# Unit 10's state sums and scores in block 3's third visit, and two visits in block 4

## The chip, the core and the metric

The kernel runs on one core of one Trainium2 chip. The core has five engines with a queue each: TensorE (PE in the profile), VectorE (DVE), ScalarE (ACT), GpSimd (POOL) and SyncE (SP), which here issues almost all DMAs. The metric is the device time of one execution in microseconds (us). Before the change its median over three runs is 198.28 us (198.15 to 198.75).

## The reference

Two stages follow each other. The first is a recurrent attention with decay (4 batches, 8 heads, 768 steps, heads of 64), the second a two-layer network with a PReLU (3072 tokens, width 512, inner width 2048):

```python
for t in range(S):
    state = gamma[None, :, None, None] * state + np.einsum('bhd,bhe->bhde', k[:, :, t], v[:, :, t])
    y[:, :, t] = scale * np.einsum('bhd,bhde->bhe', q[:, :, t], state)
...
x = np.ascontiguousarray(attn_out.transpose(0, 2, 1, 3)).reshape(B * S, H * D)
...
h = x @ w_in
g = np.maximum(h, 0.0) + alpha * np.minimum(h, 0.0)
return (g @ w_out).astype(np.float32)
```

## The kernel before

The tokens are cut into 12 units of 256 (three to a batch), and two units make a block of 512 tokens, so blocks 0 to 5. The attention of a unit is done in chunked form: products of k and v give the sums that move the state on (state sums), products of k and q give the scores within a chunk, which are masked, and then both are applied (`halves_out`) to give the unit's output y, which ScalarE copies from PSUM into `xT`, the input of the network.

Everything is ordered by hand: each engine runs its queue in the order in which the code emits it. For block n, the first layer is a generator `ffn1(n)` of 16 turns. A turn is four matmuls (128x512) into one PSUM bank, a ReLU on ScalarE into `hm` (three buffers) and a `scalar_tensor_tensor` on VectorE into `gt`. Turns alternate between the lower and the upper half of the inner width: turn 14 makes `gt[7]`, turn 15 `gt[15]`. After turn 7 and after turn 15, VectorE makes sums of `gt` (`g_sums`), two instructions each time, for a second layer that needs seven products instead of eight (`ffn2_seven`, a generator of 7 x 16 matmuls of 128x256; the products are called ox and oy after their banks). `tick(gen, m)` emits the next m matmuls of a generator with what belongs to them.

The loop over n (line 1188 on) runs the first layer of block n with the preparation of the next block's units u0 = 2(n+1) and u1 = u0 + 1 beside it, and then the second layer of block n with the attention of these two units in between. The preparation of a unit is, on GpSimd, two rescales (k and q, from float32 to float16 with the decay, `rescale`) and a cast of v (`cast_v`); on SyncE's queue a transposing DMA (`turn_dma`), the next loads (`load`, four DMAs each for k and v, one for q) and two small DMAs that move half of q (`move_q`). The first rescale is made to wait (`behind`) for the last sum of `gt` of the block before (`gate`).

From unit 6 on (`MID`), the attention goes to TensorE in three visits, small matmuls of 64x64 tiles between the large ones:

1. after 16 matmuls of the second layer: the state sums of both units (`halves_mm`) and the scores of u0 (`half_mm`);
2. after 40 more: the output of u0 (`halves_out`) and the scores of u1;
3. after 24 more: the output of u1. Then `begin(n + 1)` emits the first four matmuls of the next block's first layer; in its first turn `ffn1` takes the two units one at a time, so that these four need only u0's output. The 32 matmuls that remain of the second layer follow.

Between the visits VectorE and GpSimd carry the state on (`middle`, `behind_middle`), VectorE masks the scores (`half_masks`), and GpSimd and ScalarE copy the states to where the matmuls read them (`middle_copy`, `state_copy`; part 0 is GpSimd's, part 1 ScalarE's). Block 2 has units 6 and 7, block 3 units 8 and 9, block 4 units 10 and 11. Block 5 has no units beside it and a first layer of its own (`ffn1_mixed`).

In the trace, L632 are the first layer's matmuls, L857 the second layer's, L284 the state sums, L345 the scores, L384 and L398 the outputs; L648 and L650 are a turn's ReLU and PReLU, L613 the sums of `gt`; L185, L201 and L205 are rescale, cast and transpose; L159 and L165 the loads, L220 `move_q`; L301, L312, L313 the state, L356 the masks; L329, L333, L450, L452 the copies; L881 an addition at the end of a product.

Of the kernel before, what the change touches and what calls it, by code (L numbers as in the profile page):

```python
# [22 lines left out]
def kernel(  # L23
# [22 lines left out]

    SPLIT = 4
    MID = 6
    U = 256
    UPB = S // U  # L50
    NU = B * UPB
# [130 lines left out]
    def rescale(eng, u, t, h0, h1):  # L182
        kdq = unit(u)[0]
        at = OQ if t else (O2 if u >= SPLIT else 0)
        return eng.tensor_tensor(  # L185
            out=kdq[:, t, :, h0:h1, :].rearrange("p r h d -> p h r d"),
            in0=staged[u]["kq"[t]][:, h0:h1, :].rearrange("p h (r d) -> p h r d", r=2),
            in1=tab[:, at + 2 * h0 : at + 2 * h1]
            .rearrange("p (h r) -> p h r", r=2)
            .unsqueeze(3)  # L190
            .to_broadcast([128, h1 - h0, 2, D]),
            op=MULT,
        )
# [419 lines left out]
        last_g.append(nc.vector.tensor_tensor(out=o, in0=a, in1=b, op=op))  # L613
        return last_g[-1]

    def ffn1(n, banks, apart=0):


        turns = [(f, 2, ul, ul + 1) for ul in range(2) for f in range(0, apart, 2)]
        rest = range(apart, NFT)  # L620
        if apart == 0:
            rest = [f + x for f in range(HF) for x in (0, HF)]
        turns += [(f, 1, 0, 2) for f in rest]
        gt = None
        for i, (f0, nf, lo, hi) in enumerate(turns):
            hps = ps(banks[i % len(banks)], "hps").rearrange("p (f t) -> p f t", f=nf)
            parts = [(f, lo, hi) for f in range(nf)]
            if n > 1 and i == 0:
                parts = [(0, 0, 1), (0, 1, 2)]
            for f, ul, uh in parts:  # L630
                for hp in range(4):
                    nc.tensor.matmul(  # L632
                        out=hps[:, f, U * (ul - lo) : U * (uh - lo)].rearrange(
                            "p (u t) -> p u t", t=U
                        ),
                        lhsT=w_in_all[:, hp, 128 * (f0 + f) : 128 * (f0 + f) + 128],
                        rhs=xT[n][:, ul:uh, hp, :],
                        start=(hp == 0),
                        stop=(hp == 3),
                    )  # L640
# [7 lines left out]
            nc.scalar.activation(out=hm, in_=hps, func=RELU, bias=0.0, scale=-1.0)  # L648
            for f in range(nf):
                nc.vector.scalar_tensor_tensor(  # L650
                    out=gt[:, f0 + f, U * lo : U * hi],
                    in0=hm[:, f, :],
                    scalar=oma_sb[:, f0 + f : f0 + f + 1],
                    in1=hps[:, f, :],
                    op0=MULT,
                    op1=ADD,
                )
# [520 lines left out]
    BANKS5 = (7, 4, 7, 3, 6, 0, 4, 7)  # L1178

    def begin(n):  # L1180
        if n + 1 < NBLK:
            gen = ffn1(n, (6, 2, 3, 1, 0, 7, 5, 4, 6, 1, 0, 4, 5, 7, 6, 1))
        else:
            gen = ffn1_mixed(n, PLAN5, BANKS5)
        tick(gen, 4)
        return gen

    for n in range(1, NBLK):
        more = n + 1 < NBLK
        u0 = 2 * (n + 1)  # L1190
        if n > 1:
            gen = begun
            if more:
                for u in (u0, u0 + 1):
                    i = rescale(G, u, 0, 0, 8)
                    if u == u0:
                        behind(i, gate)
                    rescale(G, u, 1, 0, 8)
                    turn_dma(u)
                    cast_v(G, u)  # L1200
                    if u > u0:
                        load(u + 1, "qv")
                    else:
                        load(u + 2, "k")
                    move_q(u)
                    tick(gen, 8)
            tick(gen)
            if not more:
                for i in (2, 4):
                    for lo in (0, 4):  # L1210
                        g_sums(n, i, lo, lo + 4)
                g_sums(n, 0, 0, HF)
                g_sums(n, 3, 0, HF)
        gen = ffn2_seven(n, 0, 1) if more else ffn2_seven(n, 0, 1, (2, 3, (4, 6)))
        if more and u0 >= MID:
            u1 = u0 + 1
            tick(gen, 16)
            halves_mm(u0, (2, 3))
            halves_mm(u1, (6, 7))
            half_mm(u0, (4, 5))  # L1220
            m00 = middle(u0, 0)
            s00 = behind_middle(m00)
            half_masks(u0, 0)
            state_copy(s00, part=0)
            m01 = middle(u0, 1)
            s01 = behind_middle(m01)
            state_copy(s01, part=0)
            tick(gen, 8)
            middle_copy(m00, 1)
            state_copy(s00, part=1)  # L1230
            middle_copy(m01, 1)
            tick(gen, 9)
            half_masks(u0, 1)
            m10 = middle(u1, 0)
            s10 = behind_middle(m10)
            state_copy(s10, part=0)
            load(u0 + 3)
            g_sums(n, 2, 0, HF)
            tick(gen, 15)
            state_copy(s01, part=1)  # L1240
            middle_copy(m10, 1)
            tick(gen, 8)
            halves_out(u0, (2, 3))
            half_mm(u1, (4, 5))
            half_masks(u1, 0)
            state_copy(s10, part=1)
            m11 = middle(u1, 1)
            middle_copy(m11, 1)
            half_masks(u1, 1)
            s11 = behind_middle(m11)  # L1250
            state_copy(s11, part=0)
            gate = g_sums(n, 3, 0, HF)
            tick(gen, 24)
            halves_out(u1, (4, 5), evict=False)
            begun = begin(n + 1)
            take_y(u1, (0, 1))
            state_copy(s11, part=1)
            if n == NBLK - 2:
                in_sums(6, 0, V)
                in_sums(6, 1, V)  # L1260
                x_sums(n + 1, V)
                in_sums(4, 0, V)
                in_sums(4, 1, V)
        elif more:
            tick(gen, 16)
            sum_mm(u0, (2, 3))
            sum_mm(u0 + 1, (2, 3), half=1)
            score_mm(u0, 0, (4, 5))
            score_mm(u0, 1, (6, 7))
# [24 lines left out]
            state_copy(s11, part=1)  # L1294
            masks(u0 + 1, 0)
            masks(u0 + 1, 1)
            gate = g_sums(n, 3, 0, HF)
            tick(gen, 24)
            out_mm(u0 + 1, (4, 5), evict=False)
            begun = begin(n + 1)  # L1300
            take_y(u0 + 1, (0, 1))
        tick(gen)
        if n == NBLK - 2:
            in_sums(6, 2, V)
            in_sums(6, 3, V)
            in_sums(4, 2, V)
            in_sums(4, 3, V)
# [30 lines left out]
```

## Time and profile before

| | before |
|---|---|
| median of 3 runs (lowest to highest) | 198.28 us (198.15 to 198.75) |
| the profiled execution: its time | 198.86 us |
| its span, first to last instruction | 196.9 us |
| busy: TensorE, VectorE, ScalarE, GpSimd | 189.3, 156.3, 115.4, 106.1 us |
| granted TensorE clock, mean | 0.997 |
| block 3: first layer of the block / second layer with visits | 111.09 to 124.48 / 124.48 to 139.98 us |
| block 4: the same | 139.98 to 153.37 / 153.37 to 168.84 us |

The page gives busy times and shares for the whole span; the chain of waits follows the work that ended last back from its last instruction, and shows block after block when TensorE was at which line; a timeline lists the instructions of one engine in order, neighbours of one kind merged ("x8"), with the engine's idle time before them and what ended it. In rows of the timeline the first number is the start within the span, the second the duration, both in us; TensorE's starts there are about 0.17 us ahead of those of the chain, which counts from the end of the matmul before.

### The profile page before, as it was taken

Reading aid. Unit: us, or ns where it says so; the run is one execution under the profiler, and the core shown is the slowest. Engines: PE = TensorE matmul, PEld = TensorE weight load, DVE = VectorE, ACT = ScalarE, POOL = GpSimd, SP = SyncE. Lnnn points to the kernel's source line nnn. Section 1 sums busy time; section 2 is a strip of 40 time slices with the busy share of each in tenths; the row PEclk is TensorE's granted clock in tenths of the full one; section 3 lists DMA queues with packets and bytes.
Section 4 is the critical chain, followed back from the end, with each engine's and each line's share of the span. In section 5 each row is a group of like instructions: output and inputs, shape, how many; then the busy total and the mean of one; then the engine's idle time right before and its main releaser. Section 6 shows DMA issues by size and latency. Waiting matters only on the chain.

```text
span 196.9 us, 6085 instructions
## 1 busy us (share of the span) xinstructions
PE 189.3 (96%) x2529; PEld 128.8 (65%) x2529; DVE 156.3 (79%) x259; ACT 115.4 (59%) x199; POOL 106.1 (54%) x113
## 2 busy tenths in 40 slices
PE   6688999999999999999999999999999999999993
PEld 2356645568467688744688744788644788865882
DVE  7698987517698998289988389977489996999983
ACT  4458665349187668467467476467466486678110
POOL 3176897499549544970077980076970180039300
PEclk9999999999999999999999999999999999999998
DMA  5999999998879989898988899929865010400014
GB/s 156 313 317 380 374 381 377 293 180 136 211 192 200 286 197 265 213 311 175 213 203 209 256 201 191 222 65 225 256 122 126 17 57 3 160 3 0 0 65 152
DMA packets 90026, 37.92 MB, mean 193 GB/s; under 512 B 57984, under 2 KB 87696, under 8 KB 90000
## 3 DMA queue, kind: packets, MB, share of 16 engines
q1 hardware_dynamic: 88768, 36.45, 69.2%
q0 software_dynamic: 1056, 1.05, 3.6%
q8 instruction: 20, 0.33, 0.6%
q10 hardware_dynamic: 176, 0.04, 0.1%
q14 instruction: 6, 0.05, 0.1%
HBM read 27.31 MB, written 6.29 MB: 171 GB/s over the span
## 4 chain that ended last, share of the span: by engine, by line
PE 90%; SPq 4%; DMA 3%; DVE 0%; issue 0%; POOL 0%; DVEq 0%
PE hps L632 36%; PE ox L857 16%; PE oy L857 12%; PE ops L809 7%; SPq L165 4%; PE hps L719 4%; PE sp L761 3%; DMA vs<-in_v_dram 3%; PE y L533 1%; PE y L384 1%; PE trb L230 1%; PE st L284 1%; PE sca L466 1%; PE ov L857 1%; PE ow L857 1%; PE oz L857 1%
## 5 line engine op out<-in xcount | busy, mean ns | idle before, releaser
L632 PE MATMUL hps<-xT,win 128*128 128x512 f16 (+1 forms) x396 | 71.5, 338 | 0.3 <-DVE ss L423 0.3
L650 DVE SCALAR_TENSOR_TENSOR gt<-hm,oma,hps 128x512 f16<-128x512 f32 (+1 forms) x96 | 59.4, 656 | 12.1 <-issue 4.3
L648 ACT ACTIVATE hm<-hps 128x512 f32<-128x512 f32 x80 | 47.6, 597 | 24.6 <-PE hps L632 22.5
L632 PEld LDWEIGHTS <-win 128*128 128x128 f16 x396 | 38.1, 98 | 31.0 <-POOL win L978 0.4
L857 PEld LDWEIGHTS <-gs 128*128 128x128 f16 x320 | 31.0, 98 | 3.7
L857 PEld LDWEIGHTS <-gt 128*128 128x128 f16 x240 | 22.9, 98 | 4.0
L333 POOL CAST tg<-tm 64x256 f16<-64x256 f32 x12 | 4.8, 396 | 34.3 <-DVE tm L301 22.3
L185 POOL TENSOR_TENSOR kdq<-qs,tab 128x1024 f16<-128x1024 f32 (+1 forms) x12 | 20.2, 1686 | 3.0 <-DVE wsum L572 2.3
L185 POOL TENSOR_TENSOR kdq<-ks,tab 128x1024 f16<-128x1024 f32 (+1 forms) x12 | 20.2, 1686 | 2.6 <-PE y L515 2.6
L857 PE MATMUL ox<-wout,gt 128*128 128x256 f16 x144 | 17.3, 273 | 0.0
L857 PE MATMUL oy<-wsum,gs 128*128 128x256 f16 x144 | 17.2, 273 | 0.0
L556 ACT ACTIVATE xT<-y 128x512 f16<-128x512 f32 x22 | 14.9, 744 | 3.1 <-PE y L533 2.0
L201 POOL CAST vx<-vs 128x1024 f16<-128x1024 f32 (+1 forms) x13 | 12.6, 970 | 6.7 <-DMA vs<-in_v_dram 6.7
L809 PE MATMUL ops<-wout,gt 128*128 128x512 f16 x64 | 15.3, 380 | 0.0
L613 DVE TENSOR_TENSOR gs<-gt 128x1024 f16<-128x1024 f16 (+1 forms) x14 | 13.0, 934 | 0.2
L877 ACT ACTIVATE cu<-oy 128x512 f32<-128x512 f32 x10 | 6.0, 597 | 10.6 <-PE oy L857 10.1
L236 ACT ACTIVATE kq<-trb 128x1024 f16<-128x1024 f16 x8 | 8.2, 1023 | 6.3 <-PE trb L230 6.3
L313 POOL TENSOR_TENSOR tf<-ss,tab 128x256 f32<-128x256 f32 x10 | 10.3, 1028 | 2.5 <-DVE ss L312 1.3
L881 DVE TENSOR_TENSOR os<-ox,cu 128x512 f32<-128x512 f32 x5 | 3.4, 687 | 10.1 <-PE ox L857 10.1
L670 POOL TENSOR_SCALAR hn<-qc,oma 128x256 f32<-128x256 f32 x4 | 4.5, 1138 | 12.4 <-DVE qc L785 12.3
L809 PEld LDWEIGHTS <-gt 128*128 128x128 f16 x64 | 5.8, 98 | 6.0
L424 POOL TENSOR_TENSOR tf<-ss,tab 128x256 f32<-128x256 f32 x6 | 5.9, 980 | 7.1 <-DVE ss L423 7.1
(119 smaller groups left out, 293.1 us busy)
## 6 DMA issues: line engine op xcount, KB each, us to landing
qs<-in_q_dram SPq DMA_DIRECT2D x9, 512.0 KB, 5.4
ks<-in_k_dram SPq DMA_DIRECT2D x32, 128.0 KB, 3.5
vs<-in_v_dram SPq DMA_DIRECT2D x32, 128.0 KB, 4.6
early<-in_moe_w_in_dram SPq DMA_DIRECT2D x7, 512.0 KB, 7.5
out_dram<-os SPq DMA_DIRECT2D x9, 256.0 KB, 2.5
early<-in_moe_w_out_dram SPq DMA_DIRECT2D x4, 512.0 KB, 7.0
out_dram<-ot SPq DMA_DIRECT2D x4, 512.0 KB, 3.8
ks<-in_k_dram SPq DMA_DIRECT2D x6, 256.0 KB, 6.1
```

What stands on the lines that cost most here:

```text
L165: nc.sync.dma_start(out=t[nm[0]][:, h, :], in_=src[b, h, U * c : U * c + U, :].rearrange("h (p r) d -> p h (r d)", r=2),)
L185: return eng.tensor_tensor(out=kdq[:, t, :, h0:h1, :].rearrange("p r h d -> p h r d"), in0=staged[u]["kq"[t]][:, h0:h1, :].rearrange("p h ...
L201: eng.tensor_copy(out=o, in_=i)
L236: nc.scalar.activation(out=kq.rearrange("p (x a) i -> p x a i", x=4)[:, :, 2 * hh : 2 * hh + 2, :], in_=trb.rearrange("p (x a i) -> p x a ...
L313: nc.gpsimd.tensor_tensor(out=t, in0=ss, in1=dec, op=MULT)
L556: nc.scalar.activation(out=o, in_=i, func=COPY, bias=0.0, scale=1.0,)
L613: last_g.append(nc.vector.tensor_tensor(out=o, in0=a, in1=b, op=op))
L632: nc.tensor.matmul(out=hps[:, f, U * (ul - lo) : U * (uh - lo)].rearrange("p (u t) -> p u t", t=U), lhsT=w_in_all[:, hp, 128 * (f0 + f) : ...
L648: nc.scalar.activation(out=hm, in_=hps, func=RELU, bias=0.0, scale=-1.0)
L650: nc.vector.scalar_tensor_tensor(out=gt[:, f0 + f, U * lo : U * hi], in0=hm[:, f, :], scalar=oma_sb[:, f0 + f : f0 + f + 1], in1=hps[:, f, :],
L809: nc.tensor.matmul(out=opss[tq], lhsT=gt[:, ft, 128 * tq : 128 * tq + 128], rhs=w_out_all[:, ft, :], start=(ft == 0), stop=(ft == NFT - 1),)
L857: nc.tensor.matmul(out=o[1][m], lhsT=lhs(f, m), rhs=rhs(f), start=(first and f == 0 and (m == 0 or o[0] is None)), stop=(f == HF - 1), ski ...
```

## The change

Units in `AHEAD` (only unit 10) are prepared one block earlier. In block 2, `load(10, "kq")` follows unit 9's loads. Beside block 3's first layer GpSimd rescales and casts units 8, 9 and 10 (`prepare`), with unit 10's v loaded there. In block 3's third visit, unit 10's scores come ahead of unit 9's output and its state sums behind, and the state work and masks of unit 10 (`first_half`) follow on the other engines; block 4's first layer is not begun there, and its first turn is not split. Block 4 prepares unit 11 alone and has two visits: the output of unit 10 with unit 11's state sums and scores after 16 matmuls of the second layer, and the output of unit 11 after 64 more. Blocks 1, 2 and 5 keep their order but for the loads. The visits as they were are now the function `visits`, left out here.

```diff
+    AHEAD = (10,)
...
-    def ffn1(n, banks, apart=0):
+    def ffn1(n, banks, apart=0, early=False):
...
-            if n > 1 and i == 0:
+            if early and i == 0:
                 parts = [(0, 0, 1), (0, 1, 2)]
...
     def begin(n):
+        if 2 * n + 2 in AHEAD:
+            return ffn1(n, (4, 5, 6, 1, 0, 2, 3, 7, 6, 1, 0, 4, 5, 7, 6, 1))
         if n + 1 < NBLK:
-            gen = ffn1(n, (6, 2, 3, 1, 0, 7, 5, 4, 6, 1, 0, 4, 5, 7, 6, 1))
+            gen = ffn1(n, (6, 2, 3, 1, 0, 7, 5, 4, 6, 1, 0, 4, 5, 7, 6, 1), early=True)
...
+    def prepare(u0, gate):
+        def scaled(u, gate=None):
+            i = rescale(G, u, 0, 0, 8)
+            if gate is not None:
+                behind(i, gate)
+            rescale(G, u, 1, 0, 8)
+            turn_dma(u)
+
+        far, u1 = u0 + 2, u0 + 1
+        if u0 in AHEAD:
+            scaled(u1, gate)
+            cast_v(G, u1)
+            move_q(u1)
+            yield
+            return
+        scaled(u0, gate)
+        cast_v(G, u0)
+        load(far, "v" if far in AHEAD else "k")
+        move_q(u0)
+        yield
+        scaled(u1)
+        cast_v(G, u1)
+        if far in AHEAD:
+            yield
+            scaled(far)
+            cast_v(G, far)
+        else:
+            load(far, "qv")
+        move_q(u1)
+        yield
+
+    def vnext(u0):
+        if u0 + 2 in AHEAD:
+            move_q(u0 + 2)
+        load(u0 + 3)
+        if u0 + 4 in AHEAD:
+            load(u0 + 4, "kq")
...
+    def first_half(u):
+        m0 = middle(u, 0)
+        s0 = behind_middle(m0)
+        half_masks(u, 0)
+        state_copy(s0, part=0)
+        m1 = middle(u, 1)
+        s1 = behind_middle(m1)
+        half_masks(u, 1)
+        state_copy(s1, part=0)
+        return m0, s0, m1, s1
...
+                for _ in prepare(u0, gate):
                     tick(gen, 8)
+                    state_copy(begun_state.pop() if begun_state else None, part=1)
...
+            if u0 in AHEAD:
+                halves_out(u0, (2, 3))
+                halves_mm(u1, (4, 5))
+                half_mm(u1, (6, 7))
+                m10, s10, m11, s11 = first_half(u1)
+                tick(gen, 17)
+                vnext(u0)
+                middle_copy(m10, 1)
+                state_copy(s10, part=1)
+                middle_copy(m11, 1)
+                g_sums(n, 2, 0, HF)
+                tick(gen, 15)
+                state_copy(s11, part=1)
+                s11 = None
+                gate = g_sums(n, 3, 0, HF)
+                tick(gen, 32)
+            else:
+                s11 = visits(n, gen, u0)
+                gate = g_sums(n, 3, 0, HF)
+                tick(gen, 24)
+            ahead = u0 + 2 in AHEAD
+            if ahead:
+                half_mm(u0 + 2, (6, 7))
+            halves_out(u1, (4, 5), evict=ahead)
+            if ahead:
+                halves_mm(u0 + 2, (2, 3))
+                state_copy(s11, part=1)
+                m00, s00, m01, s01 = first_half(u0 + 2)
+                begun = begin(n + 1)
+                tick(gen)
+                middle_copy(m00, 1)
+                state_copy(s00, part=1)
+                middle_copy(m01, 1)
+                begun_state.append(s01)
+            else:
+                begun = begin(n + 1)
+                take_y(u1, (0, 1))
+                state_copy(s11, part=1)
```

More of the change, by code (lines that the diff above doesn't have):

```diff
@@ L1186, in begin, with visits @@
         return gen
+    def prepare(u0, gate):
[33 more added lines that the diff above has]
+            load(u0 + 4, "kq")
+    begun_state = []
+    def first_half(u):
[8 more added lines that the diff above has]
+        return m0, s0, m1, s1
+    def visits(n, gen, u0):
+        u1 = u0 + 1
+        halves_mm(u0, (2, 3))
+        halves_mm(u1, (6, 7))
+        half_mm(u0, (4, 5))
+        m00 = middle(u0, 0)
+        s00 = behind_middle(m00)
+        half_masks(u0, 0)
+        state_copy(s00, part=0)
+        m01 = middle(u0, 1)
+        s01 = behind_middle(m01)
+        state_copy(s01, part=0)
+        tick(gen, 8)
+        middle_copy(m00, 1)
+        state_copy(s00, part=1)
+        middle_copy(m01, 1)
+        tick(gen, 9)
+        half_masks(u0, 1)
+        m10 = middle(u1, 0)
+        s10 = behind_middle(m10)
+        state_copy(s10, part=0)
+        vnext(u0)
+        g_sums(n, 2, 0, HF)
+        tick(gen, 15)
+        state_copy(s01, part=1)
+        middle_copy(m10, 1)
+        tick(gen, 8)
+        halves_out(u0, (2, 3))
+        half_mm(u1, (4, 5))
+        half_masks(u1, 0)
+        state_copy(s10, part=1)
+        m11 = middle(u1, 1)
+        middle_copy(m11, 1)
+        half_masks(u1, 1)
+        s11 = behind_middle(m11)
+        state_copy(s11, part=0)
+        return s11
     for n in range(1, NBLK):
@@ L1217 @@
             tick(gen, 16)
[L1218 to L1247, printed above, removed]
```

32 lines of the change are left out of this document (10 added, 22 removed).

## The prediction

> **What bounds the kernel now.** I read the page's busy shares first, then the chain that ended last, then the timelines of VectorE, GpSimd and the DMA queue around block 3.
>
> ```profile
> span 196.9 us, 6085 instructions
> PE 189.3 (96%) x2529; PEld 128.8 (65%) x2529; DVE 156.3 (79%) x259; ACT 115.4 (59%) x199; POOL 106.1 (54%) x113
> ks<-in_k_dram SPq DMA_DIRECT2D x32, 128.0 KB, 3.5
> vs<-in_v_dram SPq DMA_DIRECT2D x32, 128.0 KB, 4.6
> ```
>
> TensorE is busy 96% of the span, and the chain of waits runs through it almost without a break from block 1 on. So the change can win only what it takes off TensorE's own sequence, and loses whatever makes TensorE wait. Rows of the chain in blocks 3 and 4 (start, duration, what):
>
> ```profile
> 111.09 13.39 PE hps L632 x64
> 124.48 1.78 PE ox L857 x16
> ...
> 127.16 1.85 PE ox L857 x16
> 129.02 1.75 PE oy L857 x16
> ...
> 135.32 0.27 PE y L384 x17
> ...
> 135.94 0.54 PE hps L632 x4
> ...
> 155.15 0.56 PE st L284 x49
> ...
> 156.02 1.85 PE ox L857 x16
> ...
> 160.49 0.38 PE y L384 x32
> ...
> 161.43 0.98 PE ox L857 x8
> ...
> 164.15 0.39 PE y L384 x32
> ...
> 164.80 0.54 PE sp L761 x4
> ```
>
> These show the three attention visits of block 4, cut into the products of the second layer: they last from 155.15 to 156.02, 160.49 to 161.43 and 164.15 to 164.80. The group of large matmuls behind each visit is about 0.10 longer than the same group elsewhere (1.85 against 1.75 for 16; 0.98 for eight, where half of 1.75 is 0.87).
>
> The second thing to see is how closely the first product of a block follows VectorE. VectorE's timeline at the end of block 3's first layer, one instruction of it by itself, and TensorE's timeline just behind:
>
> ```profile
> 119.02 0.69 DVE L613 TENSOR_TENSOR gs<-gt 128x1024 f16<-128x1024 f16 x1
> 119.75 0.69 DVE L613 TENSOR_TENSOR gs<-gs,gt 128x1024 f16<-128x1024 f16 x1
> 120.36 5.54 DVE L650 SCALAR_TENSOR_TENSOR gt<-hm,oma,hps 128x512 f16<-128x512 f32 x8
> ```
>
> ```profile
> 124.31 0.74 DVE L650 SCALAR_TENSOR_TENSOR gt<-hm,oma,hps 128x512 f16<-128x512 f32 x1
> ```
>
> ```profile
> 125.10 0.39 PE L857 MATMUL ox<-wout,gt 128*128 128x256 f16 x2
> ```
>
> Turns 8 to 15 of the PReLU follow the two sums of `gt` (the two `g_sums` after turn 7) back to back, 0.66 apart from 120.36. Turn 14 writes `gt[7]` and ends at 124.31 + 0.74 = 125.05. The eighth matmul of the first product takes `gt[7]` as weights and starts at 125.10. It already waits: the group takes 1.78 where its like take 1.75. So there is no slack; whatever delays VectorE between 119.0 and 125.0 is time lost on TensorE, one to one.
>
> **The change, part by part.** *One visit fewer.* From the code, block 4's visits hold 32 + 24 + 32 = 88, 64 + 32 = 96 and 64 small matmuls, in 0.87, 0.94 and 0.65. Slope (0.94 - 0.65) / 32 = 0.009 each, and 0.65 - 64 x 0.009 = 0.07 fixed. With the 0.10 that the next group loses, a visit costs 0.17 besides its matmuls. Unit 10's 64 matmuls (state sums and scores) move unchanged: block 3's third visit (0.62, from 135.32 to 135.94) grows by 0.58, and block 4 gets visits of 120 and 64. Gain: 0.17.
>
> *No early start of block 4's first layer.* The first turn is no longer split in eight matmuls of 256 columns, but four of 512: the same columns, so nothing. What it covered was unit 9's eviction, on ScalarE in block 3 before:
>
> ```profile
> 136.14 1.34 ACT L556 ACTIVATE xT<-y 128x512 f16<-128x512 f32 x2 [0.19 <-PE y L398]
> ```
>
> The 32 matmuls of the second layer that remain behind the visit (2 x 1.75 = 3.5) cover these 1.34; without them TensorE would wait about that long.
>
> *VectorE and ScalarE, moved.*
>
> ```profile
> L301 DVE TENSOR_TENSOR tm<-tf,st 128x256 f32<-128x256 f32 x10 | 4.2, 417 | 1.0 <-POOL tf L313 1.0
> L356 DVE TENSOR_TENSOR m<-sca,mi 128x512 f16<-128x512 f32 x6 | 4.1, 688 | 1.1 <-PE scb L345 1.1
> ```
>
> ```profile
> 140.02 0.69 DVE L881 TENSOR_TENSOR os<-ox,cu 128x512 f32<-128x512 f32 x1 [3.34 <-PE ox L857]
> ```
>
> Unit 10's two middles and two sums (0.42 each) and two masks (0.69) are 3.1 on VectorE, in the hole of 3.34 in which it waited for the last product of block 3. ScalarE's extra copies lie there too. Without that hole the first turns of block 4 would come up to 3 late, and TensorE would wait for banks. I take nothing.
>
> *The DMA queue.* k and q of unit 10 go out behind unit 9's loads in block 2.
>
> ```profile
> 101.92 2.70 SPq L159 DMA_DIRECT2D ks<-in_k_dram  x4
> 104.66 0.62 SPq L165 DMA_DIRECT2D qs<-in_q_dram  x1
> 105.33 4.03 SPq L159 DMA_DIRECT2D vs<-in_v_dram  x4
> ```
>
> ```profile
> DMA to landing us min/median/max: 4.8/5.4/6.7
> ```
>
> The last row is for all loads of q. Unit 10's four k loads are issued from 109.4, 0.67 each, q at 112.1; block 2's two stores and unit 8's transpose stand 3.3 later in the queue. With 3.5 to land (page) k is there at about 115.6, q between 116.9 and 118.8. Unit 8's transpose, issued near 113.6 instead of 112.3, is needed by TensorE near 126.8. `move_q(9)` moves behind unit 10's transpose, which waits for GpSimd until about 121.5; it is needed at 135.3. v of unit 10 takes the place that k had. In block 3 `move_q(10)`, two issues of about 0.65, pushes unit 11's loads back 1.3; GpSimd takes them up only from about 140.5. All hidden.
>
> *GpSimd.* This is the step that costs. Before, its timeline is:
>
> ```profile
> 107.83 1.90 POOL L185 TENSOR_TENSOR kdq<-ks,tab 128x1024 f16<-128x1024 f32 x1
> ...
> 116.24 1.03 POOL L201 CAST vx<-vs 128x1024 f16<-128x1024 f32 x1
> 127.74 0.39 POOL L333 CAST tg<-tm 64x256 f16<-64x256 f32 x1 [10.47 <-DVE tm L301]
> 128.28 0.61 POOL L313 TENSOR_TENSOR tf<-ss,tab 128x256 f32<-128x256 f32 x1
> ```
>
> Units 8 and 9 occupy it until 116.24 + 1.03 = 117.27, and then it is idle for over 10. Unit 10 adds two rescales of 1.90 and a cast of 1.03 in that hole: k from 117.23 to 119.13, q right behind. By length they fit. But the two sums at 119.02 and 119.75 now run beside them, and such pairs do not overlap in this trace:
>
> ```profile
> 54.95 1.22 DVE L572 TENSOR_TENSOR wsum<-wout,wsum 128x2048 f16<-128x2048 f16 x1
> 56.08 1.64 DVE L572 TENSOR_TENSOR wsum<-wout 128x2048 f16<-128x2048 f16 x1
> ```
>
> ```profile
> 55.11 1.53 POOL L424 TENSOR_TENSOR tf<-ss,tab 128x256 f32<-128x256 f32 x1 [0.22 <-DVE ss L423]
> ```
>
> ```profile
> 183.51 0.93 DVE L613 TENSOR_TENSOR gs<-gt 128x1024 f16<-128x1024 f16 x1
> ```
>
> ```profile
> 182.62 1.27 POOL L674 TENSOR_TENSOR gt<-qc,hn 128x512 f16<-128x512 f32 x1
> ```
>
> GpSimd's product, 0.61 alone, takes 1.53: it stands until VectorE's first sum ends at 54.95 + 1.22 = 56.17, then runs 0.47 to 56.64. VectorE's second sum, 1.22 alone, takes 1.64: it stands until 56.64 and ends 1.08 later, at 57.72. So one of the two works at a time, the first 0.14 of an instruction (1.22 - 1.08, 0.61 - 0.47) lies ahead of the need, and GpSimd, which had been waiting, got in between two VectorE instructions that follow each other. The second pair says the same of a sum of `gt`: 0.93 instead of 0.69, released at 182.62 + 1.27 = 183.89. The PReLU itself reads one operand from PSUM and is not slowed:
>
> ```profile
> L650 DVE SCALAR_TENSOR_TENSOR gt<-hm,oma,hps 128x512 f16<-128x512 f32 x64 | 46.2, 745 | 5.4 <-ACT hm L648 1.1
> ```
>
> Its mean over all blocks, many of them beside GpSimd's rescales, is the 0.74 of one with GpSimd idle.
>
> The sum for block 3: the first sum needs the port at 119.02 + 0.14 = 119.16, just after k's rescale ends (119.13), and ends at 119.71. q's rescale waits for it and runs 1.90 - 0.14 = 1.76, to 121.47. The second sum waits for that and ends 0.69 - 0.14 = 0.55 later, at 122.02. Turn 8 starts 0.08 before that end, as in the rows (120.36 against 119.75 + 0.69): at 121.94, 1.58 late. Queued behind it on VectorE are turns 8 to 15; for those wait ScalarE (three `hm` buffers) and the first product. Turn 14 ends at 126.63, and the eighth matmul starts 1.58 late. Turn 14's bank is freed by turn 8 at 121.94 + 0.74 = 122.68; TensorE wants it two turns before 124.48, at 122.76 (a turn is 0.86: 13.39 for fifteen and a half), so nothing is added there. Lower bound: nothing, if VectorE keeps the port. Upper bound: GpSimd takes the port first at 119.1 and again between the sums (q's rescale, then the cast): the second sum ends near 123.1, 2.7 late. I take 1.58, since the rows of 55 to 57 show the turns alternating.
>
> The Trainium skill, page "SBUF — State Buffer", section "SBUF: two separate sides", has this as an exclusive lock on a port pair, held for the whole instruction by whichever starts first, and taken by a VectorE instruction with two SBUF inputs against GpSimd; the trace agrees (1.64 instead of 1.22). The page puts a start at about 115 ns after the release; followed by the whole 0.69, the second sum would end at 122.28, an estimate that makes the stall 1.84 and the time 199.9 instead of 199.7.
>
> Total: 1.58 - 0.17 = 1.41 on the profiled execution, whose span is 196.9 and whose own time is 198.86 (1.96 outside the span, unchanged). It stands 0.58 over the median 198.28; the difference carries over: 198.28 + 1.41 = 199.7. In block 4 GpSimd has only unit 11: it starts after unit 10's last copy, some 5 behind the visit at 135.3, and takes 4.8, to about 145. The sums there start later, so nothing is lost:
>
> ```profile
> 147.91 0.69 DVE L613 TENSOR_TENSOR gs<-gt 128x1024 f16<-128x1024 f16 x1
> ```
>
> **Rivals.** *q of unit 10 comes late* (the other side). If it lands after about 119.7, the second sum takes the port at 119.8 ahead of the rescale, which then runs beside turns 8 to 11 that do not mind. Only the visit is left: 198.28 - 0.17 = 198.1. For it: the DMA engines are busy there. Against: it needs 7.6 from the issue where all loads of q took 4.8 to 6.7.
>
> *VectorE keeps the port* between its two sums, since the second is issued before the first ends. Then TensorE loses 0 to 0.1: 198.1 to 198.2. Against it stands the row of 56.08; it is one instance for this order.
>
> *GpSimd gets in twice*: 198.28 + 2.7 - 0.17 = 200.8. For it: the first sum and q's rescale want the port within 0.1 of each other. Against: v of unit 10, issued near 116 to 118.7, needs 4.6 (page) to land, after 122, so the cast is not there to get in.
>
> *The visit does more than it says*: a gain above 0.6 would need three times the fixed part of a visit; no row speaks for it.
>
> **How the numbers follow.** A change within 0.3% (0.6) is about what a measurement of this kernel cannot tell from none. Forecast 0.62, with its own range 199.2 to 200.1 (GpSimd first at 119.1 with no cast between gives a delay of about 1.8). GpSimd twice, 0.09. Another stall that I did not find, 0.03. Late q 0.09, VectorE keeping the port 0.12: both the same time as before. Faster by over 0.3%: 0.05. So slower 0.74, same 0.21, faster 0.05. The range 198.0 to 200.4 takes in the two cases without a stall and leaves out 200.8 and what is faster.
>
> **What would show it.** In the profile after: GpSimd's third pair of rescales in block 3 begins near 117.2, and the one of q takes some 2.4 instead of 1.9. One of the two sums near 119 takes over 2 instead of 0.69. The first product of block 3 takes about 3.4 instead of 1.78, released by VectorE's `gt`. Block 4 has two visits, and its stretch from the first product to the last is about 0.75 shorter, of which 0.58 came back in block 3. If the sums still take 0.69 and the first product 1.78, the forecast is wrong at the port; if the product is 1.78 though a sum is long, it is wrong in the slack.

## The result, and the profile after

| | before | after |
|---|---|---|
| median (lowest to highest) | 198.37 us (198.15 to 199.1) | 200.15 us (199.85 to 200.25) |
| profiled execution: time, span | 198.86, 196.9 us | 200.23, 198.3 us |

The ratio on record is 1.0079, 95% interval 1.006 to 1.0098, which is 1.57 us (1.2 to 1.9); the medians differ by 1.78. 1.41 was forecast. (The ratios here and below are not the quotients of the medians, and leave out one execution of experiment 5, at 202.02 us, that fell in a slower state.) Line numbers after are higher by one (L614 the sums, L633 and L858 the two layers). The profiled executions differ by only 1.37, because the start-up left block 3's first layer 0.54 earlier after (its first matmul at 110.39 against 110.93). From the start of that matmul to the start of the last one of the program it is 82.44 us before and 84.39 after, +1.95; this stretch is what the comparisons below use, called "the stretch", since it is free of the start-up.

TensorE's timeline at the beginning of block 3's second layer, after:

```profile
121.18 2.89 PE L633 MATMUL hps<-xT,win 128*128 128x512 f16 x12
123.91 1.20 PE L858 MATMUL ox<-wout,gt 128*128 128x256 f16 x7
126.15 1.16 PE L858 MATMUL ox<-wout,gt 128*128 128x256 f16 x9 [1.03 <-DVE gt L651]
```

Seven matmuls, then a wait for `gt[7]`, then nine. The visit behind the group begins at 127.23, so the group takes 3.32 where it took 1.88 by the same starts (124.31 to 126.19): +1.44, at the place that was forecast. VectorE and GpSimd in the same stretch of time, after:

```profile
118.48 0.69 DVE L614 TENSOR_TENSOR gs<-gt 128x1024 f16<-128x1024 f16 x1
119.20 2.27 DVE L614 TENSOR_TENSOR gs<-gs,gt 128x1024 f16<-128x1024 f16 x1
121.40 5.35 DVE L651 SCALAR_TENSOR_TENSOR gt<-hm,oma,hps 128x512 f16<-128x512 f32 x8
126.78 0.69 DVE L614 TENSOR_TENSOR gs<-gt 128x1024 f16<-128x1024 f16 x1
127.51 1.41 DVE L614 TENSOR_TENSOR gs<-gs,gt 128x1024 f16<-128x1024 f16 x1
128.84 0.41 DVE L302 TENSOR_TENSOR tm<-tf,st 128x256 f32<-128x256 f32 x1
```

```profile
115.62 1.03 POOL L202 CAST vx<-vs 128x1024 f16<-128x1024 f32 x1
118.76 2.17 POOL L186 TENSOR_TENSOR kdq<-ks,tab 128x1024 f16<-128x1024 f32 x1 [2.11 <-DMA ks<-in_k_dram]
120.89 2.35 POOL L186 TENSOR_TENSOR kdq<-qs,tab 128x1024 f16<-128x1024 f32 x1
127.05 1.32 POOL L202 CAST vx<-vs 128x1024 f16<-128x1024 f32 x1 [3.81 <-DMA vs<-in_v_dram]
```

A sum that takes over 2 where it took 0.69 is read here as one that stands at the port, which experiments 7 and 8 test: the second sum waits for the rescale of k that began inside the first sum, and ends 0.54 after that rescale (119.20 + 2.27 = 121.47; 118.76 + 2.17 = 120.93). Turn 8 starts at 121.40; without a stall it would start at 120.36 - 0.54 = 119.82. That is 1.58 late. A second sum is long too: the one at 127.51, 1.41, beside the cast of unit 10's v; the state's first instruction behind it (128.84) is 0.72 later for it.

SyncE's queue after (start, duration, from the timeline of the DMA queue):

```profile
110.53 3.85 SPq L160 DMA_DIRECT2D ks<-in_k_dram  x4
114.42 0.62 SPq L166 DMA_DIRECT2D qs<-in_q_dram  x1
...
116.29 5.47 SPq L206 DMA_TRANSPOSE kq<-kdq  x1
121.81 2.65 SPq L160 DMA_DIRECT2D vs<-in_v_dram  x4
```

And the chain of waits, from the wait ahead of the fourth product of block 3 on:

```profile
125.95 5.46 DMA kq<-kdq
131.41 0.59 ACT os L878
132.00 0.04 issue
132.04 1.03 PE ox L858 x8
...
136.79 0.14 PE sca L346
...
138.07 1.85 PE oy L858 x16
...
141.67 13.81 PE hps L633 x64
155.49 1.78 PE ox L858 x16
157.27 0.38 PE y L385 x32
...
158.48 1.85 PE ox L858 x16
...
165.57 0.37 PE y L385 x32
...
166.21 0.54 PE sp L762 x4
```

The chain puts a transpose (`kq<-kdq`) ahead of ScalarE's copy at 131.41, which frees the bank, since the two fall together. ScalarE's own queue shows no wait there:

```profile
130.96 0.41 ACT L330 ACTIVATE tg<-tm 64x256 f16<-64x256 f32 x1
```

This state copy ends at 131.37 and the copy starts at 131.40, 0.03 later, as before (129.38 + 0.41 = 129.79, then 129.82). So the copy was late because the state work in front of it was.

Block 4 has two visits (157.27 to 158.48, 165.57 to 166.21). Its second layer takes 14.76 from the first product to the last, 0.71 less than the 15.47 before by the same starts. Block 3's third visit lasts from 136.79 to 138.07 and grew by 0.66. The +1.95 of the stretch, by TensorE's starts:

| place on TensorE | us |
|---|---|
| block 3, turn 14 waits for its bank | +0.14 |
| block 3, first product waits for `gt[7]` | +1.44 |
| block 3, first visit | +0.10 |
| block 3, fourth product waits for a bank (ScalarE's copy at 131.41) | +0.30 |
| block 3, third visit | +0.66 |
| block 4, first layer | -0.02 |
| block 4, second layer | -0.71 |
| sum | +1.91 |

### The profile page after: what moved, and what is told of

It reads as the page before. It is cut to its first block, busy times and chain, and to the rows that moved or that the text cites. A ratio compares the mean times of both kernels' runs of the same rounds, so it can differ in the third digit from the quotient of the medians.

```text
span 198.3 us, 6079 instructions
## 1 busy us (share of the span) xinstructions
PE 190.2 (96%) x2525; PEld 128.8 (65%) x2525; DVE 158.6 (80%) x259; ACT 115.1 (58%) x199; POOL 106.7 (54%) x113
## 4 chain that ended last, share of the span: by engine, by line
PE 75%; SPq 12%; DMA 8%; POOL 1%; issue 1%; ACT 1%; DVE 0%; POOLq 0%
PE hps L633 28%; PE ox L858 13%; PE oy L858 10%; PE ops L810 7%; SPq L160 6%; SPq L166 4%; PE hps L720 3%; PE sp L762 3%; DMA early<-in_moe_w_in_dram 3%; DMA kq<-kdq 3%; DMA ks<-in_k_dram 2%; PE y L534 1%; POOL kdq L186 1%; PE trb L231 1%; PE sca L467 1%
## 5 line engine op out<-in xcount | busy, mean ns | idle before, releaser
L633 PE MATMUL hps<-xT,win 128*128 128x512 f16 (+1 forms) x392 | 71.4, 340 | 0.3 <-POOL win L979 0.2
L633 PEld LDWEIGHTS <-win 128*128 128x128 f16 x392 | 37.8, 98 | 31.4 <-issue 0.6
L858 PEld LDWEIGHTS <-gs 128*128 128x128 f16 x320 | 31.0, 98 | 4.0 <-issue 0.3
L858 PEld LDWEIGHTS <-gt 128*128 128x128 f16 x240 | 22.8, 98 | 5.5 <-DVE gt L651 1.6
L186 POOL TENSOR_TENSOR kdq<-qs,tab 128x1024 f16<-128x1024 f32 (+1 forms) x12 | 20.7, 1724 | 3.1 <-DVE wsum L573 2.3
L858 PE MATMUL ox<-wout,gt 128*128 128x256 f16 x144 | 17.6, 273 | 1.1 <-DVE gt L651 1.0
L858 PE MATMUL oy<-wsum,gs 128*128 128x256 f16 x144 | 17.2, 273 | 0.0
L614 DVE TENSOR_TENSOR gs<-gt 128x1024 f16<-128x1024 f16 (+1 forms) x14 | 13.0, 934 | 0.2
L314 POOL TENSOR_TENSOR tf<-ss,tab 128x256 f32<-128x256 f32 x10 | 9.4, 945 | 2.5 <-DVE ss L313 1.3
L979 POOL CAST win<-early 128x1024 f16<-128x1024 f32 (+1 forms) x8 | 7.5, 934 | 3.5 <-DMA early<-in_moe_w_in_dram 3.5
L425 POOL TENSOR_TENSOR tf<-ss,tab 128x256 f32<-128x256 f32 x6 | 5.8, 972 | 6.2 <-DVE ss L424 6.1
```

Of the source, the lines that this page charges most:

```text
L186: return eng.tensor_tensor(out=kdq[:, t, :, h0:h1, :].rearrange("p r h d -> p h r d"), in0=staged[u]["kq"[t]][:, h0:h1, :].rearrange("p h ...
L314: nc.gpsimd.tensor_tensor(out=t, in0=ss, in1=dec, op=MULT)
L633: nc.tensor.matmul(out=hps[:, f, U * (ul - lo) : U * (uh - lo)].rearrange("p (u t) -> p u t", t=U), lhsT=w_in_all[:, hp, 128 * (f0 + f) : ...
L858: nc.tensor.matmul(out=o[1][m], lhsT=lhs(f, m), rhs=rhs(f), start=(first and f == 0 and (m == 0 or o[0] is None)), stop=(f == HF - 1), ski ...
```

## The experiments

**1. The rescales of unit 10 behind the sums.** The changed kernel with one edit: the first of the two rescales waits for the second sum after turn 7.

```diff
         if far in AHEAD:
             yield
-            scaled(far)
+            yield
+            yield
+            scaled(far, last_g[-1])
             cast_v(G, far)
```

> The changed kernel, but unit 10's first rescale waits for the two sums of gt after turn 7 of block 3, so that GpSimd's rescales run behind them and not between them. Port theory (VectorE's second sum stands until GpSimd's rescale is done): that sum takes 0.69 instead of 2.27, the first product of block 3 about 1.8 instead of 3.3, turn 14 no longer waits for its bank; 1.58 come off 200.15, and the cast of v still meets the second pair of sums: 198.6 (198.3 to 198.8). DMA theory (unit 10's early loads hold up transposes and v, and that is the loss): nothing of it is moved earlier, so about 200.1. Load theory (GpSimd simply has 4.8 us more to do before the first visit of block 3): the same work lies later now, so 200.1 or more.

Measured: 198.92 us (single runs 198.0 to 200.65), ratio to before 1.002 (0.9995 to 1.0044); the time is 0.1 above the range expected. The timelines of VectorE and GpSimd, and the chain:

```profile
118.45 0.69 DVE L614 TENSOR_TENSOR gs<-gt 128x1024 f16<-128x1024 f16 x1
119.18 0.69 DVE L614 TENSOR_TENSOR gs<-gs,gt 128x1024 f16<-128x1024 f16 x1
```

```profile
119.95 1.90 POOL L186 TENSOR_TENSOR kdq<-ks,tab 128x1024 f16<-128x1024 f32 x1 [3.31 <-DVE gs L614]
121.81 1.90 POOL L186 TENSOR_TENSOR kdq<-qs,tab 128x1024 f16<-128x1024 f32 x1
```

```profile
123.91 1.78 PE ox L858 x16
```

The same work, begun 1.2 us later: both sums take 0.69, both rescales 1.90 (beside turns 8 to 13, which are not slowed: the eight turns take 5.54, as before), the first product 1.78 as before. So the order of the two engines there, and not the amount of work, is what the change pays for. The stretch is 82.36 here, 0.08 under before; the measured time does not resolve that.

**2. The cast of unit 10's v moved too**, behind the sums after turn 15, with the gate of 1 (`cast_v(G, u0 + 2)` after `g_sums(n, 2, 0, HF)`).

> As the run before, and the cast of unit 10's v moves behind GpSimd's state work of block 3's first visit, away from the pair of sums after turn 15. Port theory: the fourth sum takes 0.69 instead of 1.41, the wait of 0.3 before the fourth product of block 3 goes, and what is left of the change is one visit less: 198.37 - 0.17 = 198.2 (198.0 to 198.5). DMA theory: about 200.1. Load theory: GpSimd's state work in block 3's second visit now comes up to 1 later, 198.5 to 199.5.

Measured: 198.88 us, ratio 1.0018 (0.9994 to 1.0041). That is above the 198.0 to 198.5 expected. Both pairs of sums take 0.69, and the stretch is as long as before (0.01 more); the time is not to be told from 1, where the cast found its v early (landed at 123.20) and was done before the sums after turn 15.

**3. The cast moved alone**, with the rescales where the change has them.

> The changed kernel with only the cast of unit 10's v moved behind GpSimd's state work of block 3's first visit; the rescales stay ungated. Port theory: the long sum after turn 7 stays (about 2.2) and the long one after turn 15 goes; 0.3 to 0.4 come off: 199.8 (199.6 to 200.0). If the two collisions do not add (VectorE late by the first one only): 200.1.

Measured: 200.18 us, ratio 1.0079 (1.0056 to 1.0102). In the trace the wait ahead of the fourth product is gone and the stretch is 84.00, 0.39 less than after; the time, above the 199.6 to 200.0 expected, does not show it, so the share of the cast rests on the trace alone. This trace also has the order that the prediction had forecast: k's rescale ends at 118.63, just as the first sum starts, and q's, which waited for its load, stands between the sums. GpSimd, and VectorE:

```profile
116.74 1.89 POOL L186 TENSOR_TENSOR kdq<-ks,tab 128x1024 f16<-128x1024 f32 x1
119.01 2.06 POOL L186 TENSOR_TENSOR kdq<-qs,tab 128x1024 f16<-128x1024 f32 x1 [0.38 <-DMA qs<-in_q_dram]
```

```profile
119.33 2.28 DVE L614 TENSOR_TENSOR gs<-gs,gt 128x1024 f16<-128x1024 f16 x1
121.53 5.34 DVE L651 SCALAR_TENSOR_TENSOR gt<-hm,oma,hps 128x512 f16<-128x512 f32 x8
```

Block 3 starts 0.41 before that of the trace before, so turn 8 is 121.53 - (120.36 - 0.41) = 1.58 late, as after, with another rescale in the gap.

**4. Only the early preparation.** Unit 10 is loaded, rescaled and cast early as in the change, but the visits of blocks 3 and 4 stay as before.

> Unit 10 is loaded, rescaled, transposed and cast early as in the changed kernel, but block 3's third visit and block 4's three visits are as in the kernel before. Port theory: the whole loss is here, and the saving of a visit is not: 200.15 + 0.17 = 200.3 (200.0 to 200.6). If the loss came from the moved visit (unit 10's state work and copies in front of block 4): 198.4.

Measured: 200.88 us, ratio 1.0115 (1.0091 to 1.0138): the loss is there without the moved visit, and somewhat larger than expected. In this run both sums were held:

```profile
118.95 1.06 DVE L615 TENSOR_TENSOR gs<-gt 128x1024 f16<-128x1024 f16 x1
120.05 2.27 DVE L615 TENSOR_TENSOR gs<-gs,gt 128x1024 f16<-128x1024 f16 x1
```

k's rescale ended at 119.46, inside the first sum's wait; q's, ready at 119.45, stood between the sums. How much is lost thus hangs on when the loads land, within some tenths of a microsecond.

**5. Smaller pieces.** Unit 10's two rescales as eight of two heads each.

```diff
         def scaled(u, gate=None):
-            i = rescale(G, u, 0, 0, 8)
-            if gate is not None:
-                behind(i, gate)
-            rescale(G, u, 1, 0, 8)
+            step = 2 if u in AHEAD else 8
+            for t in range(2):
+                for h in range(0, 8, step):
+                    i = rescale(G, u, t, h, h + step)
...
```

> The changed kernel, but unit 10's two rescales are cut into four instructions of two heads each (eight in all, about 0.6 each, together some 0.8 longer than before); nothing is gated. Port theory with turns (each sum of VectorE waits for at most one instruction of GpSimd): the sum that took 2.27 takes 1.2 or less, the first product of block 3 is 0.8 to 1.2 shorter: 199.1 (198.8 to 199.5). Load theory (the added time on GpSimd counts): 200.2 to 200.9. If GpSimd, once it has the port, keeps it over instructions: 200.2.

Measured: 200.67 us, ratio 1.0081 (1.0054 to 1.0108). More pieces were expected to help, and by the median did not. The runs spread from 198.99 to 202.02, five of the twelve below 199.9; the one traced read 200.75, and what happened at the port in the short ones is not known. VectorE and GpSimd of the one traced:

```profile
118.29 3.40 DVE L614 TENSOR_TENSOR gs<-gt 128x1024 f16<-128x1024 f16 x1
121.72 0.69 DVE L614 TENSOR_TENSOR gs<-gs,gt 128x1024 f16<-128x1024 f16 x1
```

```profile
116.53 2.32 POOL L186 TENSOR_TENSOR kdq<-ks,tab 128x256 f16<-128x256 f32 x4
118.81 2.32 POOL L186 TENSOR_TENSOR kdq<-qs,tab 128x256 f16<-128x256 f32 x4
```

The first sum asks at 118.29, during the fourth piece, and gets nothing until the eighth has ended at 121.13: VectorE came in at none of the four boundaries between. The engines do not simply alternate, and the stall grew instead of shrinking: turn 8 is 2.71 late (122.33, where 120.36 - 0.74 would be its time, as block 3 starts 0.74 earlier than before).

**6. VectorE's sums moved instead**: the two sums after turn 7 of block 3 joined to those after turn 15, so that no sum stands ahead of turns 8 to 15.

> The changed kernel, but in block 3 the two sums of gt after turn 7 are not made there: they are joined to the two after turn 15 (two instructions of 1.22). GpSimd's work, the DMAs and the visits are those of the changed kernel. Port theory: turns 8 to 15 run on without a gap, the first product of block 3 takes 1.75 and the loss there is gone; the sums end 0.4 to 1.4 later (v's cast may meet them), of which up to 0.4 reaches TensorE in front of the fourth product: 198.6 (198.2 to 199.0). DMA and load theory: nothing of theirs is changed, and VectorE's sums cost what they did: about 200.1.

Measured: 199.75 us (single runs 198.89 to 201.48), ratio 1.0055 (1.0029 to 1.0081). The wait in front of the first product is gone, but about 1.2 is still lost, further on, where at most 0.4 was expected. From the chain:

```profile
125.44 1.89 DVE gs L614
...
131.05 0.61 ACT os L879
131.70 1.03 PE ox L859 x8
```

The doubled sums now run into the cast of v (125.20 to 126.24 on GpSimd), the state work begins behind them, ScalarE's state copies with it, and the copy that frees a bank for the fourth product stands behind those. A sum taken out of one queue position has to be paid at the next.

**7. The suspected cost alone.** The kernel before, with two products of a rescale's size on GpSimd behind unit 9's cast, into a scratch tile that nobody reads.

```diff
                     cast_v(G, u)
+                    if u == 9:
+                        scr = sbp.tile([128, 2, H, 2 * D], F16, tag="scr", name="scr")
+                        for t in range(2):
+                            G.tensor_tensor(out=scr[:, t] ..., in0=staged[u]["k"] ..., in1=tab[:, O2 : O2 + 16] ..., op=MULT)
```

> The kernel before, with two more instructions on GpSimd alone: behind unit 9's cast, two products of the size of a rescale (unit 9's k by the same table into a tile that nothing reads). No load, transpose or visit is moved. Port theory: the second of them stands between the two sums after turn 7 of block 3, VectorE is 1.6 late, TensorE waits 1.4 to 1.6 in the first product and 0.1 at turn 14: 198.5 + 1.6 = 200.1 (199.8 to 200.4). DMA theory, and load theory (GpSimd is idle there until 127): 198.5.

Measured: 200.24 us, ratio 1.0078 (1.006 to 1.0097): a loss as large as the change's, with nothing of the change but two GpSimd instructions. Here it is the first sum that is held, by the second product, and turn 8 is 121.41 - (120.36 - 0.66) = 1.71 late. The sum in question, and the first product:

```profile
118.36 2.40 DVE L613 TENSOR_TENSOR gs<-gt 128x1024 f16<-128x1024 f16 x1
```

```profile
126.16 1.16 PE L857 MATMUL ox<-wout,gt 128*128 128x256 f16 x9 [1.03 <-DVE gt L650]
```

**8. The same place, nothing read.** As 7, with two memsets (128x2048, float16, 1.80 each at 116.73 and 118.59).

> As the run before, but the two added instructions of GpSimd are memsets of 128x2048 in float16 (about 2 us each), which write SBUF and read nothing. If what the sums wait for is a port by which both engines read: 198.5, and the two sums keep 0.69. If any instruction of GpSimd that touches SBUF holds VectorE's sums up: about 200.

Measured: 198.62 us, ratio 1.0006 (0.9986 to 1.0026).

```profile
118.54 0.69 DVE L613 TENSOR_TENSOR gs<-gt 128x1024 f16<-128x1024 f16 x1
119.27 0.69 DVE L613 TENSOR_TENSOR gs<-gs,gt 128x1024 f16<-128x1024 f16 x1
```

GpSimd was about as busy as in 7, and the sums were not held. The memset reads nothing from SBUF, so the two runs point to GpSimd's reading as what shuts VectorE out, though a memset differs from a product in its kind too. In the Trainium skill, page "SBUF — State Buffer", section "SBUF: two separate sides", a VectorE instruction with two SBUF inputs conflicts only with a GpSimd instruction that reads SBUF; experiments 7 and 8 agree (2.40 against 0.69).

**9. Four products instead of two**, to see who goes next.

> The kernel before with four products of the rescale's size (128x1024, float32 to float16, all inputs long in SBUF) on GpSimd behind unit 9's cast, instead of two; they write a scratch tile that nobody reads, so the output is the same. Theory A (whoever was ready first goes first: all four products are ready before the first sum of gt asks near 118.4, so all four go ahead of it): GpSimd runs from about 116.5 to 123.9 without being disturbed, the first sum takes over 5 us, the second 0.69, turn 8 comes about 5 late, 203 to 204.5 us. Theory B (turns alternate, one GpSimd instruction between two of VectorE, as in the prediction): the first sum waits for the product that runs, the second for one more, turns 8 to 15 beside the other two: turn 8 comes 1.9 to 3.0 late, 200.2 to 201.6 us, both sums long.

Measured: 205.17 us, ratio 1.0344 (1.0328 to 1.0359); theory A's trace, and a median a little above it. GpSimd, VectorE, TensorE, and the table by stretches (total, PE, PEld, DVE, ACT and POOL busy, granted clock, DMA share, GB/s):

```profile
116.27 7.48 POOL L1204 TENSOR_TENSOR scr<-ks,tab 128x1024 f16<-128x1024 f32 x4
```

```profile
118.06 6.24 DVE L613 TENSOR_TENSOR gs<-gt 128x1024 f16<-128x1024 f16 x1
```

```profile
125.73 3.16 PE L632 MATMUL hps<-xT,win 128*128 128x512 f16 x8 [3.94 <-DVE gt L650]
```

```profile
125.70:129.00 3.30, 3.27 (x11) 1.35 (x11) 3.30 (x6) 2.46 (x5) 0.00 (x0) 0.60 1.14 236
```

The sum, asked for at 118.06, waits for all four. The stretch is 5.65 longer than before.

**10. The two gates, and unit 10's k and q loaded in block 3** where the kernel before loads k, to give block 2's stores and unit 8's transpose their places in the queue back. This was the version that might beat both.

> The changed kernel with the rescales of unit 10 behind the sums after turn 7 of block 3, the cast of its v behind the sums after turn 15, and its k and q no longer loaded in block 2 but in block 3, where the kernel before loads k; v right behind. Theory: nothing now stands between VectorE's sums and the port, and unit 8's transpose and block 2's stores have their old place in the queue, so what is left is the saving of one visit, 0.17 to 0.2: 198.2 to 198.5 us beside a kernel before of 198.3 to 198.6. Rival (the late landing of the transposes and loads in block 3 costs something that the two gated kernels still carried): 198.0 or less. Rival (the state work of unit 10 beside the end of block 3 costs as much as the visit saves): 198.5 to 198.9.

Measured: 198.97 us, ratio 1.0019 (0.9996 to 1.0041). Above the 198.2 to 198.5 expected, and neither better than 1 and 2 nor to be told from the kernel before. Its stretch, 83.13, holds a pause of 0.56 in the third visit that the profile puts down to no releaser.

**11 and 12. Who goes next, timed.** The kernel before with three products, the third behind ScalarE's ReLU of turn 8 (11) or of turn 9 (12), so that it becomes ready only after the sum has asked.

```diff
+            if n == 3:
+                while (3, 9) not in relus:
+                    tick(gen, 1)
+                behind(extra(scr, 0, tab_src), relus[3, 9])
             tick(gen)
```

> The kernel before with three products of the rescale's size on GpSimd behind unit 9's cast in block 3; the first two wait for nothing, the third waits for ScalarE's ReLU of turn 8, which ends near 119.3, that is after VectorE's first sum of gt has asked for the port (near 118.4) and before GpSimd's second product ends (near 120.2). The output is the same. One look, for its trace. Theory A (whoever was ready first goes first): the first sum waits for the second product only and takes about 2.4 us, the third product then goes next, as it was ready before the second sum asked, and the second sum takes about 2.4 too; turn 8 about 2.7 late. Rival (GpSimd keeps the port as long as its queue holds an instruction that could start): the first sum waits for the third product as well and takes about 4.2, the second 0.69.

> As the kernel with the third product behind ScalarE's ReLU of turn 8, but behind the ReLU of turn 9, which ends near 119.9, some 0.9 after VectorE's first sum of gt has asked (near 119.0) and some 0.9 before GpSimd's second product ends (near 120.9). One look, for its trace. Theory A (whoever was ready first goes first): the first sum waits for the second product only and takes about 2.4 to 2.6 us; the third product, ready before the second sum asks, goes next, so the second sum takes about 2.3; turn 8 starts where it did with three products, near 123.9. Rival (GpSimd goes on as long as its next instruction could start when the one before ends): the first sum waits for the third product as well, 4.3, and the second takes 0.69.

Measured: 202.48 and 202.37 us, one run each, beside 198.2 for the kernel before. In 11 the ReLU ended at 119.08, only 0.05 after the sum's start, too near to tell. In 12 (VectorE, ScalarE, GpSimd):

```profile
118.81 4.37 DVE L614 TENSOR_TENSOR gs<-gt 128x1024 f16<-128x1024 f16 x1
123.22 0.69 DVE L614 TENSOR_TENSOR gs<-gs,gt 128x1024 f16<-128x1024 f16 x1
```

```profile
119.13 0.60 ACT L649 ACTIVATE hm<-hps 128x512 f32<-128x512 f32 x1 [0.27 <-PE hps L633]
```

```profile
117.02 5.61 POOL L1182 TENSOR_TENSOR scr<-ks,tab 128x1024 f16<-128x1024 f32 x3
```

The third product is ready at 119.73, 0.9 after the sum has asked, and still goes first. Theory A falls; the rival stands: GpSimd went on here as long as its next instruction could start when the one before ended. The profile after does not fit it, which "The rule of turns" below takes up.

## Why the prediction was right, and where not

*What bounds it, and where it breaks.* Right. Turns 8 to 15 have no slack: 1.58 lost by VectorE are 0.14 + 1.44 on TensorE. The prediction said that nothing is added at turn 14's bank; 0.14 came there, out of the same 1.58 (its first matmul waits until turn 8 has ended). The work that moved to the end of block 3 on VectorE and ScalarE, taken as nothing, cost nothing there: block 4's first layer is unchanged (-0.02).

*The port, the term of 1.58.* Right in place, size and cause. Turn 8 is 1.58 late, after and in experiment 3; experiment 7 makes such a stall out of two GpSimd instructions alone, experiments 1 and 8 take it away. The order forecast (k's rescale just done, q's between the sums) is that of experiment 3, but not of the profile after: there k's rescale stood between, and q's was held itself (2.35). It came out alike because either way one rescale is passed on its way from the first sum's end to the second. In that execution the size was in part luck. Both loads were late: q landed only at 119.86, where the prediction's own limit for "late q" is 119.7 - 0.54 = 119.16. Had k been there at 115.6 as forecast, the second sum would by the prediction's reasoning have gone ahead of q's rescale, with no stall.

*"All hidden", on the DMA queue.* Wrong. k was to land near 115.6; one of its issues took 1.73 and its last part landed 4.86 after the issue, at 118.60. Unit 8's transpose took 5.47 in the queue (2.30 before), so v's loads went out only from 121.81. In block 3 this was paid once: v's cast met the last sum (1.41 instead of 0.69), and through the state work and ScalarE's copies the fourth product of block 3 waited 0.30. "The cast is not there to get in" held only for the sums after turn 7.

*The visit, -0.17.* Too good. The two stretches that it trades, -0.71 and +0.66, leave -0.05 after, and the first visit is 0.10 longer, for a cause that stays open. The term was mis-sized in the larger visits: block 3's third takes 1.28 where 0.62 + 0.58 = 1.20 was forecast, and block 4's first 1.21 where the same slope gives 1.15. With the stall gone the whole stretch is 0.08 shorter than before in experiment 1 and 0.01 longer in 2, and the three gated kernels read 198.88 to 198.97 against 198.54 to 198.58. Their intervals all hold 1, and no time here shows a saving.

*The sum.* 1.58 - 0.17 = 1.41 was forecast. The trace gives 1.58 + 0.30 + 0.10 - 0.05 - 0.02 = 1.91, the medians 1.78. The terms that the forecast lacks are the cast's collision and the visit's smaller worth.

*The other estimate.* The Trainium skill's page "SBUF — State Buffer", in its section "SBUF: two separate sides", led to a stall of 1.84 by putting a start 115 ns after the release, a figure that the page gives for GpSimd held by VectorE and not the other way round. Here the held sum ended 0.54 after k's rescale, less than its 0.69 alone, which is the row-based 0.55; the measurement decides for 1.58.

*The rivals.* "VectorE keeps the port" did not come about. "Late q" had its condition in the profile after but not its outcome, because k was late too and reached the port while the first sum had it. "GpSimd gets in twice" happened in part in experiment 4 (both sums held, 1.06 and 2.27), where turn 8 came 1.96 late (122.25, with block 3 starting 0.07 earlier than before).

*The rule of turns.* The sentence that carried 1.58, turns alternate, is half right. Wherever GpSimd waited while a sum had the port, it came in before VectorE's next sum: in the rows from 55 to 57 of the profile before, in the profile after, and in experiments 3 and 4. The other way round it is not general. In 5, 9 and 12 GpSimd passed four, two and one of its own boundaries with VectorE waiting. In the profile after, VectorE did come between two rescales, though q had landed (issue at 114.42, landing at 119.86) before k's rescale ended at 120.93; in experiment 4 it did so too, when k's rescale had ended at 119.46. What tells these apart stays open. In the profile after, k's rescale had itself been held by a sum, and in 5, 9 and 12 the instruction that ran had not. In experiment 4 k's rescale had not been held either (1.90), but q, landed at 119.45, left a gap: its rescale began at 119.52, 0.06 after the end of k's, where GpSimd's rescales otherwise begin some 0.04 before that end. None of this was tried.

## What to carry to other kernels

An engine's idle hole is not free for work that shares a port with an instruction on the bounding chain: look for the two-input VectorE instructions inside the hole, and for what is queued behind them. Put a wait in, so that the added work starts behind them (experiment 1: 1.2 us later, no loss); cutting it into pieces did not help in the one trace of it. And a visit less, on an engine that is 96% busy, was worth under 0.1 us.

## What the runs showed of the hardware

- A row of GpSimd instructions that read SBUF kept VectorE's sum out until the last had ended: 3.40 us (eight pieces), 6.24 (four products), against 0.69. The memsets of experiment 8 did not.
- A wait of 3.94 us on TensorE was followed by a granted clock of 0.60 over the next 3.3 us, eight matmuls in 3.16 where eight take 1.89 after the wait of 2.07 in experiment 12. The Trainium skill, page "TensorE: Matmul & The Clock Gate", section "Part 1: The HAM clock gate (the "warmup" mystery)", has the array at half clock after idling; the trace of experiment 9 agrees. The slow stretch costs 3.16 - 1.89 = 1.27 in the traced execution, which read 203.62 us; three of the other four, at 205.17 to 205.71, show a mean clock of 0.983 against 0.992 here.
- The same transpose (unit 8's) took 2.30 us in the queue before, and 5.47 after, behind five more loads. The loads are not all of it: it took 4.10 with the same loads in experiment 1, and 3.67 in experiment 10, without them in front.
